# A DeltaNet recurrence and a low-rank mixer on one core: inverse times v added up in PSUM, 15 products for 18 in two more half chunks

## The chip, the cores and the metric

One Trainium2 chip, one of its cores. The metric is the device time of one execution in microseconds (us); less is better.

## The reference

Two blocks run one after the other. The first is a recurrence over 768 positions for 4 batches and 8 heads of 48 columns; its output, with the heads side by side (384 columns), is the input of a mixer.

```python
k_n = k / (norm(k) + 1e-6)
for t in range(768):                       # state: 4 x 8 x 48 x 48, starts at 0
    y[t]  = q[t] @ state
    v_old = state.T @ k_n[t]
    state = state + beta[t] * outer(k_n[t], v[t] - v_old)
x = y with heads side by side              # 4 x 768 x 384
u = x + (x.transpose @ U @ V).transpose    # U: 768 x 32, V: 32 x 768
out = u + relu(u @ w_ch1) @ w_ch2          # 384 -> 1536 -> 384
```

All is fp32.

## The kernel before

**The recurrence** is done in chunks of 64 positions, 12 chunks a batch, 6 chunks ("unit" n) at a time for all 8 heads. Within a chunk the kernel solves a triangular system: it forms the products of keys (`grams`, `products`), inverts 32x32 diagonal blocks on VectorE column by column (`blocks`, lines 824 and 830), and joins them into the inverse of a 64x64 block with small matmuls (`joins`, lines 881 to 942). `recur(b)` then uses that inverse `zt`. `prepare` multiplies it by the keys (line 1044, to `kq`) and by v (line 1055, back into `vn`), three chunks at a time. Each chunk c then takes four steps that hang on one another: 8 matmuls of `kq` with the state (line 1093); a VectorE subtraction z = `vn` - that product (line 1106); 8 matmuls of keys with z (line 1121); a VectorE addition to the state (line 1132). Beside the chain, `outputs` makes y from the queries with the state and the masked products with z (lines 1004 and 1018), which ScalarE copies to `X` (line 988). These matmuls use 64x64 tiles of TensorE's array, those of `joins` 32x32, those of the mixer 128x128.

**The mixer** goes over a batch in three chunks of 256 positions, (b, i). `front` adds the low-rank part and turns u to `ut` (lines 1488 to 1534). `wide` makes the 1536 hidden features: 6 pairs of feature tiles, each with 3 matmuls a tile of 256 columns (line 1596), and ScalarE applies the ReLU (line 1553). `narrow` multiplies by w_ch2 (line 1761) in 7 products for 8, from sums that VectorE makes (lines 1676 and 1683), and `gather` adds the results to `X` (line 1689). The last batch has its own code with 15 products for 18 in both layers, over 768 positions at once (lines 1402 and 1891).

**15 products for 18.** The first layer on 3 by 3 blocks of weights and 3 by 2 blocks of u (128 by 128 each) is 18 block products. A bilinear scheme does it with 15, from sums of weight blocks (`weight_sums`) and of u blocks (`tokens`). `FAST` names the chunks that do this: before, (2, 2) alone, both halves h of the features. `CHAINS` lists the products e in two chains; each runs through one PSUM region, where a product is added to the sum so far, and after each product the sum is read (`seen`): a ScalarE copy for some (line 1645 or 1640), a VectorE addition or subtraction for the others (line 1651). So the next product of a chain has to wait for the read. Each half h has one PSUM bank, with its two chains in the two halves of it, and every product is 2 matmuls of 128 columns (line 1626).

**The order.** The coroutines above don't choose when they run. `ORDER` is a long list that gives each step of each coroutine its place, and `run` emits the instructions in that order; every engine works its own queue in it. Costs in calls such as `op("pe", 0.23, "Q", ...)` are left from the planner that made the list. PSUM has four pairs of banks (`pair`); two banks of one of them become the mixer's (`mix`) later. Input loads go through the SP and GpSimd queues, weights through SP.

Of the kernel before, what the change touches and what calls it, by code (L numbers as in the profile page):

```python
# [8 lines left out]
FP32 = mybir.dt.float32  # L9
# [8 lines left out]
BK = 32  # L18
# [9 lines left out]
def kernel(  # L28
# [116 lines left out]
    add_up b0 i0 f00: 594 612 668; add_up b0 i0 f03: 632 645 667; add_up b0 i1 f00: 793 820 841; add_up b0 i1  # L145
    f03: 846 859 861; add_up b0 i2 f00: 1012 1041 1060; add_up b0 i2 f03: 1040 1042 1046; add_up b1 i0 f00: 1151
    1161 1173; add_up b1 i0 f03: 1208 1213 1214; add_up b1 i1 f00: 1347 1371 1372; add_up b1 i1 f03: 1357 1375
    1378; add_up b1 i2 f00: 1505 1574 1594; add_up b1 i2 f03: 1592 1595 1598; add_up b2 i0 f00: 1684 1685 1725;
    add_up b2 i0 f03: 1726 1728 1731; add_up b2 i1 f00: 1843 1849 1866; add_up b2 i1 f03: 1865 1871 1876; add_up
    b2 i2 f00: 2108 2110 2111; add_up b2 i2 f03: 2107 2109 2112; blocks n0: 61 73 75 76 82 84 86 88 89 91 93 94  # L150
    96 97 103 110 114 122; blocks n1: 143 157 160 163 173 175 179 192 201 206 208 212 213 215 218 219 226 229;
    blocks n2: 479 498 510 513 514 518 520 524 526 528 529 532 536 538 539 541 542 544; blocks n3: 691 708 710
    711 714 716 718 720 721 722 733 740 744 748 752 755 756 760 768 769 771 785 788 792 794 797 798 799 800 801
    802 824 825 826; blocks n4: 937 941 942 944 948 951 964 965 966 967 975 977 979 1011 1017 1022 1031 1036
    1039 1043 1045 1062 1078 1081 1082 1093 1099 1104 1117 1120 1122 1125 1127 1129; blocks n5: 1144 1152 1155
    1156 1159 1160 1165 1167 1168 1169 1187 1207 1230 1231 1233 1239 1241 1242 1243 1256 1260 1261 1265 1266
    1272 1274 1277 1278 1280 1313 1319 1350 1354 1355; blocks n6: 1469 1475 1476 1477 1478 1480 1481 1482 1483
    1499 1502 1516 1524 1526 1539 1548 1552 1558 1573 1588 1590 1597 1599 1603 1605 1606 1612 1617 1622 1623
    1635 1637 1638 1645; blocks n7: 1674 1686 1688 1691 1692 1693 1694 1705 1707 1709 1716 1721 1722 1746 1749
    1753 1756 1766 1774 1783 1784 1786 1795 1804 1822 1824 1825 1826 1827 1828 1830 1831 1851 1852; channels b0  # L160
    i0 e0: 546 547; channels b0 i0 e1: 551 552; channels b0 i0 e2: 553 555; channels b0 i0 e3: 556 567; channels
    b0 i0 e4: 568 588; channels b0 i0 e5: 597 600; channels b0 i1 e0: 738 743; channels b0 i1 e1: 759 761;
    channels b0 i1 e2: 775 778; channels b0 i1 e3: 796 805; channels b0 i1 e4: 822 829; channels b0 i1 e5: 830
    832; channels b0 i2 e0: 924 927; channels b0 i2 e1: 932 934; channels b0 i2 e2: 936 939; channels b0 i2 e3:
    960 972; channels b0 i2 e4: 992 994; channels b0 i2 e5: 995 1030; channels b1 i0 e0: 1110 1112; channels b1
    i0 e1: 1115 1116; channels b1 i0 e2: 1130 1132; channels b1 i0 e3: 1142 1146; channels b1 i0 e4: 1153 1154;
    channels b1 i0 e5: 1172 1180; channels b1 i1 e0: 1257 1258; channels b1 i1 e1: 1273 1286; channels b1 i1 e2:
    1287 1295; channels b1 i1 e3: 1299 1311; channels b1 i1 e4: 1315 1334; channels b1 i1 e5: 1340 1342;
    channels b1 i2 e0: 1451 1461; channels b1 i2 e1: 1465 1484; channels b1 i2 e2: 1485 1488; channels b1 i2 e3:
    1490 1501; channels b1 i2 e4: 1518 1519; channels b1 i2 e5: 1535 1549; channels b2 i0 e0: 1643 1647;  # L170
    channels b2 i0 e1: 1652 1672; channels b2 i0 e2: 1673 1677; channels b2 i0 e3: 1701 1702; channels b2 i0 e4:
    1703 1706; channels b2 i0 e5: 1710 1711; channels b2 i1 e0: 1797 1798; channels b2 i1 e1: 1813 1814;
    channels b2 i1 e2: 1834 1837; channels b2 i1 e3: 1839 1840; channels b2 i1 e4: 1841 1844; channels b2 i1 e5:
    1845 1846; cut f0 f00 k0 to1: 2205; cut f0 f00 k1 to0: 2236; cut f0 f00 k1 to1: 2179; cut f0 f00 k2 to0:
    2246; cut f0 f00 k2 to1: 2245; cut f1 f03 k0 to1: 2293; cut f1 f03 k1 to0: 2301; cut f1 f03 k1 to1: 2295;
    cut f1 f03 k2 to0: 2312; cut f1 f03 k2 to1: 2311; cut f2 f06 k0 to1: 2214; cut f2 f06 k1 to0: 2235; cut f2
    f06 k1 to1: 2239; cut f2 f06 k2 to0: 2234; cut f2 f06 k2 to1: 2244; cut f3 f09 k0 to1: 2252; cut f3 f09 k1
    to0: 2292; cut f3 f09 k1 to1: 2294; cut f3 f09 k2 to0: 2306; cut f3 f09 k2 to1: 2303; diagonals n0 h0: 188
    190 191 195 210 222; diagonals n0 h1: 167 169 171 176 181 186; diagonals n1 h0: 312 315 319 336 343 353;
    diagonals n1 h1: 290 292 303 338 349 358; diagonals n2 h0: 598 599 622 628 634 638; diagonals n2 h1: 647 651  # L180
    672 697 703 724; diagonals n3 h0: 863 890 891 892 893 899; diagonals n3 h1: 879 880 881 889 931 933;
    diagonals n4 h0: 1171 1178 1183 1189 1198 1199; diagonals n4 h1: 1163 1210 1211 1232 1246 1247; diagonals n5
    h0: 1373 1387 1392 1396 1419 1436; diagonals n5 h1: 1395 1407 1410 1415 1416 1417; diagonals n6 h0: 1699
    1734 1735 1736 1787 1788; diagonals n6 h1: 1655 1681 1764 1789 1790 1791; diagonals n7 h0: 1874 1879 1885
    1889 1906 1909; diagonals n7 h1: 1854 1856 1873 1888 1902 1905; fifteen b2 i2 h0 k0: 1953 1962 1977 1987
    2007 2016 2042 2055 2088; fifteen b2 i2 h0 k1: 1956 1991 2004 2008 2054 2082; fifteen b2 i2 h1 k0: 1960 1976
    2005 2011 2028 2063 2073 2089 2096; fifteen b2 i2 h1 k1: 1990 2017 2051 2072 2083 2097; front b0 i0: 495 502
    503 515 516 519; front b0 i1: 523 561 591 602; front b0 i2: 636 652 678 682; front b1 i0: 1056 1064 1074
    1080 1102 1105; front b1 i1: 1106 1114 1131 1164; front b1 i2: 1196 1219 1228 1238; front b2 i0: 1593 1596
    1601 1619 1627 1628; front b2 i1: 1632 1671 1690 1700; front b2 i2: 1737 1748 1762 1769; front b3 i0: 2094  # L190
    2095 2102 2103 2114 2117; front b3 i1: 2119 2121 2123 2124; front b3 i2: 2127 2129 2131 2132; gather b0 i0
    h0 c0 k0: 677; gather b0 i0 h0 c0 k1: 680; gather b0 i0 h0 c1 k6: 737 871; gather b0 i0 h1 c0 k2: 693;
    gather b0 i0 h1 c0 k5: 734 926; gather b0 i0 h1 c1 k3: 706; gather b0 i0 h1 c1 k4: 715; gather b0 i1 h0 c0
    k0: 862; gather b0 i1 h0 c0 k1: 847; gather b0 i1 h0 c1 k6: 916 925; gather b0 i1 h1 c0 k2: 873; gather b0
    i1 h1 c0 k5: 913 1034; gather b0 i1 h1 c1 k3: 876; gather b0 i1 h1 c1 k4: 887; gather b0 i2 h0 c0 k0: 1044;
    gather b0 i2 h0 c0 k1: 1071; gather b0 i2 h0 c1 k6: 1109 1428; gather b0 i2 h1 c0 k2: 1072; gather b0 i2 h1
    c0 k5: 1111 1450; gather b0 i2 h1 c1 k3: 1079; gather b0 i2 h1 c1 k4: 1087; gather b1 i0 h0 c0 k0: 1206;
    gather b1 i0 h0 c0 k1: 1216; gather b1 i0 h0 c1 k6: 1251 1780; gather b1 i0 h1 c0 k2: 1220; gather b1 i0 h1
    c0 k5: 1249 1445; gather b1 i0 h1 c1 k3: 1229; gather b1 i0 h1 c1 k4: 1240; gather b1 i1 h0 c0 k0: 1377;
    gather b1 i1 h0 c0 k1: 1388; gather b1 i1 h0 c1 k6: 1446 1664; gather b1 i1 h1 c0 k2: 1408; gather b1 i1 h1  # L200
    c0 k5: 1441 1630; gather b1 i1 h1 c1 k3: 1412; gather b1 i1 h1 c1 k4: 1413; gather b1 i2 h0 c0 k0: 1589;
    gather b1 i2 h0 c0 k1: 1604; gather b1 i2 h0 c1 k6: 1636 1832; gather b1 i2 h1 c0 k2: 1608; gather b1 i2 h1
    c0 k5: 1639 1781; gather b1 i2 h1 c1 k3: 1613; gather b1 i2 h1 c1 k4: 1620; gather b2 i0 h0 c0 k0: 1727;
    gather b2 i0 h0 c0 k1: 1733; gather b2 i0 h0 c1 k6: 1782 1968; gather b2 i0 h1 c0 k2: 1752; gather b2 i0 h1
    c0 k5: 1794 2309; gather b2 i0 h1 c1 k3: 1754; gather b2 i0 h1 c1 k4: 1768; gather b2 i1 h0 c0 k0: 1898;
    gather b2 i1 h0 c0 k1: 1897; gather b2 i1 h0 c1 k6: 1951 2197; gather b2 i1 h1 c0 k2: 1915; gather b2 i1 h1
    c0 k5: 1957 2369; gather b2 i1 h1 c1 k3: 1918; gather b2 i1 h1 c1 k4: 1938; gather b2 i2 h0 c0 k0: 2116;
    gather b2 i2 h0 c0 k1: 2120; gather b2 i2 h0 c1 k6: 2142 2367; gather b2 i2 h1 c0 k2: 2126; gather b2 i2 h1
# [1813 lines left out]
```

## Time and profile before

| | |
|---|---|
| three runs | 587.42, 589.74, 590.85 us; median 589.74 |
| profiled execution | 591.4 us, of which the core's span 589.5 |
| mean granted TensorE clock | 0.939 of full speed |
| busy: TensorE matmuls (PE) | 552.9 us, 94% |
| busy: weight loads (PEld), beside the matmuls | 479.6 us, 81% |
| busy: VectorE (DVE) | 449.8 us, 76% |
| busy: ScalarE (ACT) | 221.8 us, 38% |
| busy: GpSimd (POOL) | 133.1 us, 23% |
| DMA | 36.23 MB, mean 61 GB/s |

A group's row reads: line, engine, operation, out<-in by the program's names, shapes, xcount | busy us, mean ns of one | idle time of the engine before them and what ended it. A row of waits reads: who <- whom, us in total, times, longest. A row of the chain or the timeline begins with its start in us from the span's start and its length. A busy PE is one whose pipeline holds a matmul.

### The profile page before, as it was taken

To read this page: it belongs to the slowest core of one execution; us is meant where nothing else is said; L and a number is where in the kernel's file an instruction comes from. 1 tells how busy PE (TensorE), PEld (TensorE's weight loads), DVE (VectorE), ACT (ScalarE), POOL (GpSimd) and SP (SyncE) were. 2 spreads that over 40 slices of the span, in tenths; PEclk is the share of its full clock that TensorE was granted. 3 is DMA by queue.
4 is the path that set the end of the run, shared out by engine and by line. 5 is a ranking of instruction groups with operands and counts; after the bars stand their busy time and mean duration, and the time that the engine had idled before them with its cause. 6 is when DMAs were issued, how large, how long until landed. Compare 5 with 4: busy or idle time off the path is not lost.

```text
span 589.5 us, 23569 instructions
## 1 busy us (share of the span) xinstructions
PE 552.9 (94%) x10452; PEld 479.6 (81%) x10452; DVE 449.8 (76%) x1077; ACT 221.8 (38%) x460; POOL 133.1 (23%) x229
## 2 busy tenths in 40 slices
PE   3788886899999999999999999999999999999997
PEld 3788775688988988889989987989889777755996
DVE  3888756899999577989957489999858345799743
ACT  2846473616432632026325332143261442335100
POOL 8122034124206415032313403063310000000000
PEclk9665566999999999999999999999999999999999
DMA  9960638532206135030302403160210000100001
GB/s 143 200 158 24 217 86 186 109 94 49 37 2 121 22 65 105 12 68 15 67 19 51 85 13 72 34 130 17 68 29 4 17 4 1 40 2 0 1 27 68
DMA packets 89397, 36.23 MB, mean 61 GB/s; under 512 B 75408, under 2 KB 87056, under 8 KB 89296
## 3 DMA queue, kind: packets, MB, share of 16 engines
q1 hardware_dynamic: 80752, 24.69, 20.0%
q0 software_dynamic: 6944, 9.74, 7.7%
q8 instruction: 82, 1.34, 0.9%
q10 hardware_dynamic: 1600, 0.30, 0.3%
q14 instruction: 19, 0.16, 0.1%
HBM read 29.98 MB, written 4.72 MB: 59 GB/s over the span
## 4 chain that ended last, share of the span: by engine, by line
PE 82%; DVE 11%; issue 3%; ACT 2%; DMA 1%; SPq 0%; DVEq 0%; ACTq 0%
PE P L1761 22%; PE P L1596 20%; PE P L1891 7%; PE P L1402 7%; PE P L721 4%; PE P L1626 3%; PE P L1093 2%; DVE xt L830 2%; DVE prod L824 2%; PE P L1121 2%; PE P L895 2%; PE P L881 2%; PE P L1044 2%; PE P L1055 2%; PE P L1018 1%
## 5 line engine op out<-in xcount | busy, mean ns | idle before, releaser
L1596 PE MATMUL P<-ut,w_sb 128*128 128x256 f32 x576 | 133.4, 385 | 0.0
L1596 PEld LDWEIGHTS P<-ut,w_sb 128*128 128x128 f32 x576 | 106.6, 190 | 15.4 <-issue 0.6
L1761 PE MATMUL P<-w_sb,hs 128*128 128x192 f32 x540 | 94.5, 329 | 0.0
L1761 PEld LDWEIGHTS P<-w_sb,hs 128*128 128x128 f32 x540 | 87.4, 190 | 2.7 <-issue 1.8
L830 DVE TENSOR_TENSOR xt<-xt,prod 128x112 f32<-128x112 f32 (+21 forms) x200 | 64.6, 323 | 6.9
L824 DVE TENSOR_TENSOR prod<-gs,xt 128x112 f32<-128x112 f32 (+21 forms) x200 | 63.2, 316 | 3.5
L988 ACT COPY X<-P 64x192 f32<-64x192 f32 x96 | 30.0, 313 | 68.0 <-PE P L1018 67.1
L1553 ACT ACTIVATE hs<-P 128x512 f32<-128x512 f32 x48 | 28.6, 597 | 64.3 <-PE P L1596 55.4
L1761 PE MATMUL P<-w_sb,S 128*128 128x192 f32 x216 | 37.7, 330 | 0.0
L576 POOL DMA_DIRECT2D slot<-in_v_dram x32 | 21.1, 666 | 73.1 <-DVE prod L824 68.6
L1761 PEld LDWEIGHTS P<-w_sb,S 128*128 128x128 f32 x216 | 34.9, 190 | 2.6 <-issue 1.2
L1689 DVE TENSOR_TENSOR X<-X,P 128x192 f32<-128x192 f32 x63 | 21.7, 348 | 17.4 <-PE P L1761 17.1
L562 POOL DMA_DIRECT2D slot<-in_k_dram x40 | 24.9, 629 | 38.8 <-DVE z L1106 37.6
L1106 DVE TENSOR_TENSOR z<-slot,P 128x192 f32<-128x192 f32 x44 | 15.5, 352 | 23.7 <-PE P L1093 23.1
L960 ACT COPY slot<-zz 32x384 f32<-32x384 f32 x64 | 32.2, 508 | 3.0 <-DVE zz L899 2.1
L721 PE MATMUL P<-slot 48*64 48x64 f32 x1536 | 32.1, 237 | 0.7 <-DVE slot L752 0.7
L721 PEld LDWEIGHTS P<-slot 48*64 48x64 f32 x1536 | 29.1, 151 | 4.2 <-issue 1.6
L967 POOL MEMSET slot<- 32x384 f32 x32 | 13.0, 411 | 83.7 <-PE P L924 64.5
L576 POOL DMA_DIRECT2D slot<-in_k_dram x44 | 29.3, 668 | 7.8 <-PE P L1121 7.6
L562 POOL DMA_DIRECT2D slot<-in_q_dram x40 | 24.5, 618 | 16.3 <-DVE slot L734 8.2
L809 POOL MEMSET xt<- 128x1056 f32 x8 | 7.9, 982 | 83.4 <-DVE zz L837 83.3
L1132 DVE TENSOR_TENSOR s<-s,P 128x192 f32<-128x192 f32 x40 | 13.9, 348 | 12.2 <-PE P L1121 11.3
(204 smaller groups left out, 1053.9 us busy)
## 6 DMA issues: line engine op xcount, KB each, us to landing
w_sb<-in_moe_w_ch_dram SPq DMA_DIRECT2D x10, 384.0 KB, 4.8
out_dram<-X SPq DMA_DIRECT2D x19, 192.0 KB, 3.4
slot<-in_k_dram SPq DMA_DIRECT2D x48, 72.0 KB, 3.7
slot<-in_k_dram POOLq DMA_DIRECT2D x44, 72.0 KB, 3.5
slot<-in_v_dram SPq DMA_DIRECT2D x32, 72.0 KB, 3.0
slot<-in_v_dram POOLq DMA_DIRECT2D x32, 72.0 KB, 3.0
X<-in_moe_w_ch_dram SPq DMA_DIRECT2D x6, 384.0 KB, 4.6
wide<-in_moe_w_ch_dram SPq DMA_DIRECT2D x6, 384.0 KB, 5.2
```

The lines of the kernel that those rows point to most:

```text
L562: queue.dma_start(out=blocked(n)[quarter(y % 4), j, g, :, 0:w], in_=src[b, 4 * g + 2 * j + par, hf * UC * L : (hf + 1) * UC * L, BK * low ...
L576: queue.dma_start(out=t[half(1 - g if name == "z" else g), :, to, 0:D], in_=src[b, 4 * g + s, hf * UC * L : (hf + 1) * UC * L, :].rearrang ...
L721: nc.tensor.matmul(p_g[half(g ^ (par * i)), par, c], kq[rows, c, j, 0, half(g)], kq[rows, c, j, i, half(g)], start=True, stop=True,)
L824: nc.vector.tensor_tensor(out=prod, in0=gb[:, :, j : j + 1, j + 1 :].to_broadcast([128, split, m, w]), in1=xb[:, :, 0:m, j : j + 1].to_bro ...
L830: nc.vector.tensor_tensor(out=xb[:, :, 0:m, j + 1 :], in0=xb[:, :, 0:m, j + 1 :], in1=prod, op=ALU.subtract,)
L960: nc.scalar.copy(pg[quarter(i), :, at, :, a : a + BK], cut(zc, h)[quarter(i)].rearrange("p r (c j) t -> p r c j t", j=2),)
L988: nc.scalar.copy(x[half(c % 2), c // 2, 4 * D * g : 4 * D * (g + 1)].rearrange("p (j r d) -> p r j d", r=2, d=D), states(p_y)[half(g)],)
L1402: nc.tensor.matmul(to, forms[h][w][:, g] if isinstance(w, str) else w1_of(*w, h)[:, g], TOKENS[t] if isinstance(t, str) else u_of(*t), sta ...
L1553: nc.scalar.activation(hs[:, fs[0] : fs[1] + 1 : fs[1] - fs[0]], p_f, ACTF.Relu)
L1596: nc.tensor.matmul(p_f[:, x], w(x, t), ut[:, t], start=(t == 0), stop=(t == KT - 1))
L1761: nc.tensor.matmul(to, of[0], of[1], start=of[2], stop=of[3], skip_group_check=True)
L1891: nc.tensor.matmul(p[:, m], a[:, h, 128 * m : 128 * m + 128], v[:, h, j], start=fresh and m == h == j == 0, stop=(j == h == 1), skip_group ...
```

## The change

- **15 products for 18 in two more half chunks.** `FAST` also names half 0 of chunks (1, 2) and (2, 1). Their other half stays with plain matmuls.
- **One line to a bank.** In the chunk (2, 2), where both halves are fast, a chain now has a bank of its own and a product is 4 matmuls over all four feature groups of both halves, read by one instruction of 512 columns. In a half-fast chunk the chains use a pair of banks, one each, and a product is 2 matmuls as before. The chains are cut differently: products 10 and 12 are in the second.
- **Inverse times v in PSUM.** For batches 1 to 3, `prepare` no longer multiplies by v. A new coroutine `values(c)` writes the inverse times v of one chunk into a PSUM pair; the matmuls with the state, with `kq` negated, are added there; ScalarE copies the sum as z. The matmuls of keys with z go into other columns of the next chunk's pair.
- **Diagonal blocks.** For units 3 to 7, `products` builds `diag` with four ScalarE copies of 32 partitions in place of a ScalarE multiplication and two VectorE operations.
- **First pair of `narrow`.** In half-fast chunks its two products are made in the other order.
- **New order.** `ORDER` is a new list.

The core of the diff, without `ORDER`:

```diff
@@ products
-                yield op("act", act(384) + 0.1, rush=True)
-                nc.scalar.mul(to, p_g[:, :, :, 0:BK], even[:, 0:1])
-                for r in range(2):
+                if n > NU * JOINT:
+                    for y in range(4):
+                        a = BK * (y % 2)
+                        yield op("act", act(384))
+                        nc.scalar.copy(to[quarter(y)], p_g[quarter(y), :, :, a : a + BK])
+                else:
+                    yield op("act", act(384) + 0.1, rush=True)
+                    nc.scalar.mul(to, p_g[:, :, :, 0:BK], even[:, 0:1])
+                for r in range(2) if n <= NU * JOINT else ():
@@ recur
+    JOINT = 1
@@ prepare
+            if n >= NU * JOINT:
+                yield op("act", act(768), give=[("pair", x)])
+                nc.scalar.mul(
+                    kq[:, cs[0] : cs[2] + 1, :, 0].rearrange("p c j (g t) -> p (c j) g t", g=2),
+                    p_k.rearrange("p g c j t -> p (c j) g t"), -1.0,
+                )
+                emitted(("ready", n, h), 0.1)
+                return
@@ recur
+        def values(c):
...
+            x = yield op("pe", 0.23, "Q", take="pair", words=32, flow=0.16)
+            sums[c] = x
+            for j, par, g in heads:
+                nc.tensor.matmul(
+                    states(pair(x)[:, :, 0 : 2 * D])[half(g ^ par), par, j],
+                    zt[half(g), par, cu, j],
+                    vn[half(g), cu, 2 * par + j],
+                    start=(j == 0),
+                    stop=(c == 0),
+                    skip_group_check=True,
+                )
...
-            if c == 0:
+            if b >= JOINT:
+                yield need(("values", b, c))
+                xb = sums[c]
+                p_b = pair(xb)[:, :, 0 : 2 * D]
+                if c > 0:
...
+                            kq[half(par, D), cu, j, 0, half(g)],
+                            states(s_old)[half(par, D), g, j],
+                            start=False,
...
+                yield op("act", act(192), give=[("pair", xb)], rush=True)
+                z = zs[c] = small.tile([128, 4, D], FP32, name="z", bufs=3)
+                nc.scalar.copy(z.rearrange("p (r j) d -> p r (j d)", r=2), p_b)
...
+                if b >= JOINT:
+                    yield need(("values", b, c + 1))
+                    p_s = pair(sums[c + 1])[:, :, 2 * D : 4 * D]
@@ fast chunks
-    FAST = {(2, 2): (0, 1)}
+    FAST = {(1, 2): (0,), (2, 1): (0,), (2, 2): (0, 1)}
     CHAINS = (
-        ((4, 0, 1, 1), (10, 2, 0, -1), (12, 1, 0, 1), (13, 1, 0, 1), (2, 1, 1, -1), (7, 0, 1, -1), (14, 2, 1, 1),
-         (5, 2, 0, -1), (11, 0, 0, 1)),
-        ((1, 1, 1, 1), (6, 0, 1, 1), (9, 1, 1, 1), (0, 1, 0, -1), (3, 2, 0, 1), (8, 2, 1, -1)),
+        ((4, 0, 1, 1), (13, 1, 0, 1), (2, 1, 1, -1), (7, 0, 1, -1), (14, 2, 1, 1), (5, 2, 0, -1), (11, 0, 0, 1)),
+        ((1, 1, 1, 1), (10, 2, 0, -1), (12, 1, 0, 1), (6, 0, 1, 1), (9, 1, 1, 1), (0, 1, 0, -1), (3, 2, 0, 1),
+         (8, 2, 1, -1)),
     )
@@ fifteen
-        def fifteen(h, k):
-            bank = h if len(quickly) == 2 else 0
+        def fifteen(k):
+            joint = len(quickly) == 2
...
-                for g in range(2):
+                if z == 0:
+                    p = (mixed(k) if joint else pair(own[0])[:, k])[:, 0 : GT * len(quickly)]
+                    p = p.rearrange("p (g n) -> p g n", n=128)
+                for g in range(2 * len(quickly)):
+                    h = quickly[g // 2]
@@ seen
-                yield op("act", act(256), rush=True)
+                yield op("act", act(n), rush=True)
                 nc.scalar.mul(to, p, float(sign))
@@ narrow
+            turns = [(1, 1), (0, 0)] if e == 0 and len(quickly) == 1 else list(enumerate(ys))
```

More of the change, by code (lines that the diff above doesn't have):

```diff
@@ L1072, in prepare @@
             emitted(("ready", n, h), 0.1)
+        sums = {}
+        def values(c):
+            n, cu = NU * b + c // UC, c % UC
+            _, _, zt, _, _, vn, _, _ = units[n]
+            yield need(
+                *[x for h in [cu // 3] for x in (("upper", n, h), ("diagonal", n, h))],
+                ("grams", n), ("scaled", n), *[("placed", b, c - 2)] * (c > 1),
+            )
[9 more added lines that the diff above has]
+                    skip_group_check=True,
+                )
+            emitted(("values", b, c))
         zs = {}
+        if b >= JOINT:
+            for c in range(NC):
+                begin(values(c), 60)
         for u in range(NU):
@@ L1618, in fifteen @@
                     *[("weights", 2 + y) for y in range(len(PAIRS))],
-                    *[("w1 sums", h)] * isinstance(w, str),
+                    *[("w1 sums", h) for h in quickly] * isinstance(w, str),
                     *[("sum", b, i, int(x[1:])) for x in [t] if isinstance(x, str)],
-                    *[("seen", b, i, h, CHAINS[k][z - 1][0])] * (z > 0),
-                    *{6: [("made", b, i, h, 13)], 13: [("made", b, i, h, 1)]}.get(e, []),
-                )
-                yield op("pe", 0.432, "F", take=("mix", bank) if z == k == 0 else None, words=8)
@@ L1625, in fifteen @@
-                for g in range(2):
+                    *[("seen", b, i, CHAINS[k][z - 1][0])] * (z > 0),
+                )
+                got = yield op(
+                    "pe", 0.432 * len(quickly), "F", words=8 * len(quickly),
+                    take=None if z or k and not joint else ("mix", k) if joint else "pair",
+                )
+                if z == 0 and not joint:
+                    own[0] = own[0] if k else got
+                if z == 0:
+                    p = (mixed(k) if joint else pair(own[0])[:, k])[:, 0 : GT * len(quickly)]
+                    p = p.rearrange("p (g n) -> p g n", n=128)
@@ L1631, in fifteen @@
                     )
-                emitted(("made", b, i, h, e))
-                begin(seen(h, e, p, r, m, sign, [("mix", bank)] * (e == 11)), 3)
-        def seen(h, e, p, r, m, sign, give):
-            to = hs[:, HF * h + r : HF * h + r + 4 : 3, 128 * m : 128 * m + 128]
+                emitted(("made", b, i, e))
+                give = [("mix", k)] if joint and e in (8, 11) else [("pair", own[0])] if e == 11 else []
+                begin(seen(e, p, r, m, sign, give), 3)
+        own = [None]
```

542 lines of the change are left out of this document (284 added, 258 removed).

## The prediction

> **What bounds the kernel now.** I read the page first (share of each engine and the chain), then the stages, then who waits for whom, then single matmuls in the timeline. All from one execution of 591.4 us: a span of 589.5 and 1.9 around it, 1.7 above the median of the runs shown (589.74). I work the sum as a difference against the profiled execution and carry it to the median.
>
> ```profile
> PE 552.9 (94%) x10452; PEld 479.6 (81%) x10452; DVE 449.8 (76%) x1077; ACT 221.8 (38%) x460; POOL 133.1 (23%) x229
> ...
> PE 82%; DVE 11%; issue 3%; ACT 2%; DMA 1%; SPq 0%; DVEq 0%; ACTq 0%
> ...
> 0.00:20.00 20.00, 9.31 (x199) 8.48 (x200) 9.21 (x30) 7.20 (x14) 14.93 (x31) 1.00 1.09 156
> ...
> 120.00:140.00 20.00, 19.74 (x456) 16.80 (x455) 19.53 (x40) 7.25 (x14) 8.38 (x14) 1.00 0.37 86
> 140.00:160.00 20.00, 20.00 (x550) 18.27 (x549) 19.50 (x45) 10.48 (x20) 5.52 (x10) 1.00 0.22 39
> ...
> 460.00:480.00 20.00, 18.46 (x566) 16.28 (x564) 8.12 (x24) 8.56 (x25) 0.00 (x0) 1.00 0.02 4
> ```
>
> The stages give busy us of PE, PEld, DVE, ACT, POOL, then the granted clock. Batch 0 of the recurrence and the weight loads fill the first 115 us with PE waiting; from 120 us on PE is busy for nearly all of every 20 us at a granted clock of 1.00. DVE is almost as full around 120 to 160. What PE still waits for after 112 us:
>
> ```profile
> PE P L1093 <- DVE s L1132: 0.8, 1, 0.8
> PE P L1531 <- DVE X L1512: 0.8, 1, 0.8
> PE P L1626 <- ACT hs L1645: 0.7, 2, 0.5
> PE P L1507 <- DVE tt L1494: 0.4, 1, 0.4
> PE P L1626 <- DVE hs L1651: 0.3, 1, 0.3
> PE P L881 <- DVE zz L837: 0.3, 1, 0.3
> PE P L1121 <- DVE z L1106: 0.3, 1, 0.3
> ...
> PEld P L1121 <- DVE z L1106: 2.9, 12, 0.4
> ```
>
> 3.6 us in all. So from 115 us on only less work on PE, or fewer breaks in it, moves the end. The orders of instructions of the two kernels are equal on PE up to this point (the first 1314 matmuls), so the first 114 us stand as they are.
>
> **The change part by part. Products.** One fp32 matmul stands in the trace as two records.
>
> ```profile
> 415.84 2.79 PE P L1596 x12
> ...
> 420.82 13.15 PE P L1596 x60
> ...
> 456.33 0.71 PE L1626 MATMUL P<-S,w_sb 128*128 128x128 f32 x4
> 457.56 1.60 PE L1626 MATMUL P<-S,w_sb 128*128 128x128 f32 x12 [0.52 <-ACT hs L1645]
> 459.10 0.45 PE L1093 MATMUL P<-s,slot 48*64 48x48 f32 x16
> 459.37 0.41 PE L1004 MATMUL P<-s,slot 48*64 48x48 f32 x16
> 459.60 0.41 PE L1018 MATMUL P<-z,slot 64*64 64x48 f32 x16
> 460.02 0.40 PE L1121 MATMUL P<-z,slot 64*48 64x48 f32 x16
> 460.35 0.71 PE L1626 MATMUL P<-S,w_sb 128*128 128x128 f32 x4
> ```
>
> From x60 and x12: (13.15-2.79)/48 = 0.216 us for a record of 256 columns. From the x12 and x4 of L1626: (1.60-0.71)/8 = 0.111 for 128 columns. Each of the two new half-fast chunks drops 18 matmuls of 256 columns (36 records, 7.8 us) and gets 30 of 128 (60 records, 6.7 us): -1.1 each, **-2.2 us**. The least is -0.7: that holds if each of the 15 runs of 8 records pays 0.1 more for its first load. The joint chunk b2 i2 keeps its 60 matmuls.
>
> The Trainium skill ("TensorEngine Tiling (Array Packing)", Instruction Overhead) speaks against more, shorter matmuls: about 60 cycles of overhead on each. At its 2.4 GHz that is 25 ns, and 48 more records would cost 1.2 us by it, so -1.0 here. The rows show 2 x 0.111 against 0.216, 6 ns a record, and I go by them.
>
> **Changes of tile size.** In the instruction orders PE goes 175 times from one tile size (128x128, 64x64, 32x32, 128x32) to another before, and 160 times after. A run of 12 records of 256 columns takes 2.79 where 12 x 0.216 is 2.59: 0.20 for its entry and exit. The small groups next to it: L1004 to L1018 is 0.23 start to start, L1121 to L1626 0.33, L1093 to L1004 0.27: 0.14 more. So 0.34 for two changes, some 0.15 for one (0.10 to 0.20): 15 x 0.15 = **-2.2 us**, all on PE's path.
>
> **One line to a bank, and the stalls of b2 i2.** A chain's product used to cover two feature groups of one half and now covers all four, so behind a product twice as much matmul time stands while its sum is read. The 0.7 and 0.3 above are PE waiting for exactly these reads; I take **-0.7**, with 0 and -1.0 as ends. A read becomes 512 wide; it is one instruction for two, so ACT and DVE lose fixed cost.
>
> **Tail.** The new order has three places where nothing stands between a matmul and the read it needs. In the first layer of the last batch, product 12 comes right behind product 10 of the same line twice; before, other lines lay between. In its second layer the last product's second half comes behind a DVE read of its first half.
>
> ```profile
> L1427 ACT ACTIVATE slot<-P 128x384 f32<-128x384 f32 x20 | 9.3, 490 | 18.5 <-PE P L1402 18.5
> L1645 ACT ACTIVATE hs<-P 128x256 f32<-128x256 f32 x10 | 3.6, 384 | 10.0 <-PE P L1626 9.2 <-ACT X L988 0.8
> L1900 DVE TENSOR_TENSOR X<-X,P 128x384 f32<-128x384 f32 x14 | 7.7, 552 | 14.7 <-PE P L1891 14.7
> L1689 DVE TENSOR_TENSOR X<-X,P 128x192 f32<-128x192 f32 x63 | 21.7, 348 | 17.4 <-PE P L1761 17.1
> ```
>
> The nearest row is the uncovered wait of L1626 above: 0.52 idle around a copy of 0.384. With 0.490 that is 0.63, twice 1.3; with a DVE read of 0.348 it is 0.49. The last read is then half as wide (0.552 to 0.348, -0.2). Together **+1.6** (1.0 to 2.2).
>
> **Recurrence, batches 1 to 3.** The inverse times v is no longer made ahead and copied (12 copies of L1068 go); 8 matmuls a chunk write it into PSUM, 8 more subtract the state's share there, and ACT copies z where DVE subtracted. PE's count is the same, 288 matmuls with v for 288. DVE loses 33 subtractions.
>
> ```profile
> L1106 DVE TENSOR_TENSOR z<-slot,P 128x192 f32<-128x192 f32 x44 | 15.5, 352 | 23.7 <-PE P L1093 23.1 <-ACT hs L1645 0.4
> L988 ACT COPY X<-P 64x192 f32<-64x192 f32 x96 | 30.0, 313 | 68.0 <-PE P L1018 67.1
> L1063 ACT COPY slot<-P 128x768 f32<-128x768 f32 x16 | 12.8, 798 | 24.8 <-PE P L1044 24.5
> L1068 ACT COPY slot<-P 128x576 f32<-128x576 f32 x16 | 10.3, 642 | 0.9 <-PE P L1055 0.7
> L1553 ACT ACTIVATE hs<-P 128x512 f32<-128x512 f32 x48 | 28.6, 597 | 64.3 <-PE P L1596 55.4 <-issue 6.7 <-DVE slot L734 2.0
> L948 ACT ACTIVATE slot<-P 32x384 f32<-32x384 f32 x32 | 15.3, 480 | 7.7 <-PE P L942 7.3
> L731 ACT ACTIVATE slot<-P,even 128x384 f32<-128x384 f32 x16 | 9.1, 582 | 27.1 <-PE P L721 26.9
> L734 DVE SCALAR_TENSOR_TENSOR slot<-P,even,slot 128x192 f32<-128x192 f32 x32 | 12.3, 412 | 7.7 <-ACT slot L731 7.6
> ```
>
> A step of the chain (state matmuls, z, S matmuls, state) is as long as before: a copy of about 0.31 for a subtraction of 0.35. DVE: -33 x 0.352 = -11.6. Units 3 to 7 also build their diagonal blocks with four ACT copies (0.48 each) in place of one ACT and two DVE (0.582, 2 x 0.412): DVE -8.2, ACT +13.4, and the block's transpose starts 1.92 - 1.41 = 0.5 later, beside work of batches that PE has queued. The new token sums and reads of the half chunks put some 14 back on DVE (about 34 operations of 0.4, between the 0.348 and 0.552 of the 192 and 384 wide forms above). Net DVE -6, ACT +20. ACT, busy for 38%, hides that, if the queue in front of z is short; PE's own sum is **0**. Its ends: -2.9, if all twelve waits of the weight load for z go, and +7.2: in ACT's new order a 768-wide copy stands straight ahead of 6 copies of z and a 512-wide ReLU ahead of 4 (6 x 0.80 + 4 x 0.60).
>
> **Sum.** -2.2 - 2.2 - 0.7 + 1.6 = **-3.5**: 587.9 for the profiled execution, 586.2 for the median. A measurement of this kernel can tell about 0.5% (2.9 us) from no change.
>
> **The rivals.** First, **slower: z waits in ACT's queue.** In the 33 steps z now stands behind ReLUs and copies of other stages; the S matmuls wait, and PE behind them in order. For it: the rows of L1063 and L1553 are two to three times a z copy. Against it: ACT is idle for 62%, DVE for 24%, so z left the fuller queue. With +7.2 the sum is +3.7, 593.4. It decides from (3.5+2.9)/33 = 0.19 us a step.
>
> Second, **DVE was holding PE back** (19.5 of 20 us in two stages): relieved of 6 us it lets the waits of 3.6 and of 2.9 go too, half of each: -6.8, 582.9. Against it: PE's waits are few as they are.
>
> Third, **the gain is given back**: a PE that is earlier waits for the block solves on DVE in 120 to 180 us, which are no shorter; 0, 589.7.
>
> Fourth, **the halves don't pay**: the 128-wide records average 0.155, as the 56 in 8.7 us of one group do, since short runs pay an entry each time:
>
> ```profile
> L1626 PE MATMUL P<-S,w_sb 128*128 128x128 f32 x56 | 8.7, 286 | 0.6 <-ACT hs L1645 0.5
> ```
>
> 120 x 0.155 = 18.6 against 15.6, +3.0 for -2.2: the sum is +1.7, 591.4, and with the upper tail (+0.6) and a 0 for the joint chunk (+0.7) +3.0, 592.7. Against it: most new runs have four matmuls next to other 128x128 matmuls, so no entry is paid.
>
> **How the numbers follow.** Forecast 0.47 (583.5 to 588.7 by itself), z on ACT 0.15, DVE relieved 0.18, given back 0.13, halves don't pay 0.07. Faster by over 0.5%, below 586.8: the second rival and 0.30 of the forecast, 0.48. Slower, above 592.7: the first and fourth, 0.22. Within: the rest of the forecast and the third, 0.30. The lower end adds the best bounds, -2.2 - 3.0 - 1.0 + 1.0 - 2.9 = -8.1: 581; the upper the z rival with the poor ends of products (-0.7), switches (-1.5), joint chunk (0) and tail (+2.2), +7.2: 597; I draw it in to 596, since they hardly all meet.
>
> **What would show it.** PE's busy time between 115 us and the end shorter by 3 to 4 us; records of the products 0.111 apart in the two half chunks; two idle gaps of some 0.6 us near the start of the last batch's first layer and one before the last matmuls; no growth of waits of the S matmuls, now for ACT. It is wrong if PE's waits after 112 us rise above 8 us: z copies queued on ACT would show it, waits for block solves the third rival, and records 0.15 apart the fourth.

## The result, and the profile after

| | before | after |
|---|---|---|
| first comparison, median (runs) | 590.36 us (8) | 587.14 us (8) |
| ratio, 95% interval | | 0.9944 [0.9917, 0.9971] |
| second comparison, median (runs) | 589.2 us (29) | 585.23 us (12) |
| ratio, 95% interval | | 0.995 [0.9925, 0.9975] |
| profiled execution, span | 589.5 us | 583.8 us |

The forecast was 586.2 us, 3.5 less than before; the two comparisons give 3.2 and 4.0 less. By the ratios that is 0.5 to 0.6%, right at the bound of what was taken as distinguishable; in both comparisons the 95% interval lies below 1. The page of the changed kernel: engines, then the chain by engine.

```profile
PE 547.7 (94%) x10500; PEld 478.3 (82%) x10500; DVE 445.6 (76%) x1049; ACT 240.0 (41%) x519; POOL 132.5 (23%) x229
...
PE 84%; DVE 8%; ACT 3%; issue 3%; DMA 1%; SPq 0%; DVEq 0%; ACTq 0%
```

PE is as full as before and still the bound. DVE is 4 us lighter, ACT 18 heavier, about as worked out (6 and 20). What PE waits for after 112 us, all rows:

```profile
PE P L1479 <- ACT slot L1504: 1.2, 2, 0.6
PE P L1673 <- ACT ut L1611: 0.9, 1, 0.9
PE P L908 <- issue: 0.6, 2, 0.3
PE P L1980 <- DVE X L1989: 0.4, 1, 0.4
PE P L1141 <- DVE s L1211: 0.4, 1, 0.4
PE P L1584 <- DVE tt L1571: 0.4, 1, 0.4
PE P L952 <- ACT zz L942: 0.3, 1, 0.3
PE P L1033 <- ACT z L1155: 0.2, 1, 0.2
```

4.4 us in all, of which the first row and the fourth are the tail's three gaps. The waits at the products of the joint chunk (L1626 before, L1711 now) are gone. z, now a copy by ACT, is waited for once, for 0.2 us. A wait for `ut` of 0.9 is new and was not foreseen; it stands at 116 us, where PE before waited 0.8 at L1531.

The starts of matmul records cut the span into stages. "Order starts to differ" is the first matmul that the new order moves; the columns "again" and "tail moved" belong to the first experiment below.

| us | before | after | again | tail moved |
|---|---|---|---|---|
| start to where the order starts to differ | 115.04 | 113.11 | 115.29 | 111.82 |
| from there to the last batch's first layer (the middle stage) | 392.22 | 386.92 | 386.66 | 387.49 |
| first layer of the last batch | 38.77 | 40.61 | 40.61 | 39.32 |
| its second layer | 38.84 | 39.55 | 39.55 | 39.55 |
| last matmul to the end | 4.61 | 3.59 | 3.60 | 3.59 |

The first line is the same instructions in every column: it ran from 110.95 to 115.29 us over the twelve executions profiled here, which is as much as the change itself. The 1.9 us that the profiled pair differ by there are no effect of the change. The middle stage repeats to about 1 us in the changed kernel (the kernel before was profiled once), and it is the one to read. Cut at its own ends, it shows what PE did in it: stage, length, then busy us of PE, PEld, DVE, ACT, POOL, granted clock, DMA; first before, then again.

```profile
115.04:507.26 392.22, 388.19 (x7557) 339.84 (x7550) 309.71 (x770) 138.18 (x291) 96.03 (x161) 1.00 0.22 45
115.29:501.95 386.66, 384.54 (x7605) 340.60 (x7598) 304.84 (x743) 157.10 (x350) 96.11 (x161) 1.00 0.22 46
```

PE is busy for 3.7 us less (3.8 in the first profile, 384.34) and idle for 2.12 us (2.58) in place of 4.03.

### The profile page after: what moved, and what is told of

Read it like the earlier page. It is cut to its first block, busy times and chain, and to the rows that moved or that the text cites. A ratio compares the mean times of both kernels' runs of the same rounds, so it can differ in the third digit from the quotient of the medians.

```text
span 583.8 us, 23666 instructions
## 1 busy us (share of the span) xinstructions
PE 547.7 (94%) x10500; PEld 478.3 (82%) x10500; DVE 445.6 (76%) x1049; ACT 240.0 (41%) x519; POOL 132.5 (23%) x229
## 4 chain that ended last, share of the span: by engine, by line
PE 84%; DVE 8%; ACT 3%; issue 3%; DMA 1%; SPq 0%; DVEq 0%; ACTq 0%
PE P L1851 20%; PE P L1673 20%; PE P L1479 7%; PE P L1980 7%; PE P L1711 5%; PE P L728 4%; PE P L1019 2%; PE P L1033 2%; PE P L1141 2%; PE P L1109 2%; PE P L908 2%; PE P L894 2%; PE P L1584 2%; PE P L1197 2%; PE P L1059 2%
## 5 line engine op out<-in xcount | busy, mean ns | idle before, releaser
L1673 PE MATMUL P<-ut,w_sb 128*128 128x256 f32 x504 | 118.0, 385 | 0.9 <-ACT ut L1611 0.9
L1673 PEld LDWEIGHTS P<-ut,w_sb 128*128 128x128 f32 x504 | 92.8, 190 | 14.3 <-ACT ut L1611 1.1
L843 DVE TENSOR_TENSOR xt<-xt,prod 128x112 f32<-128x112 f32 (+21 forms) x200 | 64.5, 323 | 6.9
L837 DVE TENSOR_TENSOR prod<-gs,xt 128x112 f32<-128x112 f32 (+21 forms) x200 | 63.5, 317 | 3.7
L1630 ACT ACTIVATE hs<-P 128x512 f32<-128x512 f32 x42 | 24.9, 597 | 33.9 <-PE P L1673 31.0
L728 PE MATMUL P<-slot 48*64 48x64 f32 x1536 | 30.7, 231 | 2.0 <-issue 1.2
L728 PEld LDWEIGHTS P<-slot 48*64 48x64 f32 x1536 | 27.7, 144 | 5.5 <-issue 2.2
L1155 ACT COPY z<-P 128x192 f32<-128x192 f32 x36 | 11.4, 317 | 43.5 <-PE P L1141 43.4
L1740 DVE TENSOR_TENSOR hs<-hs,P 128x256 f32<-128x256 f32 (+1 forms) x27 | 13.5, 507 | 17.6 <-PE P L1711 16.8
```

The source lines that it names most:

```text
L728: nc.tensor.matmul(p_g[half(g ^ (par * i)), par, c], kq[rows, c, j, 0, half(g)], kq[rows, c, j, i, half(g)], start=True, stop=True,)
L837: nc.vector.tensor_tensor(out=prod, in0=gb[:, :, j : j + 1, j + 1 :].to_broadcast([128, split, m, w]), in1=xb[:, :, 0:m, j : j + 1].to_bro ...
L843: nc.vector.tensor_tensor(out=xb[:, :, 0:m, j + 1 :], in0=xb[:, :, 0:m, j + 1 :], in1=prod, op=ALU.subtract,)
L1673: nc.tensor.matmul(p_f[:, x], w(x, t), ut[:, t], start=(t == 0), stop=(t == KT - 1))
```

## Experiments

"The changed kernel" is at 585.23 us, ratio 0.995, below. Kernels were compared with the kernel before on the same chip; its medians in the three groups were 589.2, 589.26 and 588.69.

### The tail: three exchanges in the order

> The changed kernel itself, to have it on one chip beside the others. Every reading of the change expects 0.990 to 0.998 of the kernel before (the first comparison gave 0.9944), 584 to 589 us. Its trace also tells which gaps come again: the two of about 0.6 us in the first layer of the last batch and the one of about 0.45 us before the last matmuls should, if they belong to the order and not to one execution.

> The changed kernel with three entries of its written order exchanged in the last batch, the same instructions otherwise: the third product of line f0 changes places with the quick product of f2 behind it, and the quick product of f0 comes ahead of the third product of f3, so that a product no longer takes a PSUM bank right behind the matmul whose sum ACT has still to read there. Theory of the prediction (the two gaps of 0.63 and 0.58 lie on PE's path, nothing else is late there): the two gaps go, 1.2 us shorter than the changed kernel (0.6 to 1.6), about 586 where that one has 587.1; first layer of the last batch 39.4 us instead of 40.6. Rival, the gaps are only where PE's lead over ACT is spent and come back behind another instruction: less than 0.3 us of difference, first layer 40.3 us or more.

```diff
 ORDER, by place
-2207 short f0 k3      2208 quick f2
+2207 quick f2         2208 short f0 k3
-2251 short f3 k2      2252 read e4 f3      2253 quick f0
+2251 quick f0         2252 short f3 k2     2253 read e4 f3
```

Again: 585.23 us. Moved: 583.85 us, ratio 0.9918 [0.9893, 0.9943]. The timeline of PE (start, length, engine, line, operation, shapes, records, idle before) in the changed kernel, at the start of the first layer, and at the end of the second:

```profile
501.32 0.81 PE L1479 MATMUL P<-slot,w_sb 128*128 128x384 f32 x2
502.76 2.20 PE L1479 MATMUL P<-slot,w_sb 128*128 128x384 f32 x6 [0.63 <-ACT slot L1504]
...
515.28 0.91 PE L1479 MATMUL P<-slot,w_sb 128*128 128x384 f32 x2 [0.58 <-ACT slot L1504]
...
579.60 0.92 PE L1980 MATMUL P<-w_sb,slot 128*128 128x192 f32 x4 [0.45 <-DVE X L1989]
```

With the entries exchanged the first two are gone: the records now follow without a break, here the place of the first one.

```profile
499.96 0.81 PE L1479 MATMUL P<-slot,xt 128*128 128x384 f32 x2
500.60 3.00 PE L1479 MATMUL P<-slot,w_sb 128*128 128x384 f32 x8
```

The layer falls from 40.61 to 39.32 us, 1.3 for two gaps of 0.63 and 0.58: they were on the path and nothing else stood behind them. The medians differ by 1.4, less than the intervals of the two ratios are wide, so it is the stage that shows it. This version has the lowest time here.

### The products: fewer halves, and one more

> The changed kernel with the halved products taken away again in the two chunks that the change gave them (second batch's last chunk, third batch's middle chunk): their second halves go through 18 products of 256 columns, one line to a bank, as the first halves do; 48 matmuls fewer, tile changes on PE 160 as in the changed kernel, the rest of the order as it was. Theory of the prediction (records of 0.216 and 0.111 us): 2.2 us slower than the changed kernel (0.7 to 2.9), of which up to 0.7 for VectorE or ScalarE work that is then no longer needed could be hidden; PE's busy time +2.2. Rival, the halves don't pay because short runs pay an entry each time (0.155 us a record): 3.0 us faster; halfway, 0, if half of the entries are paid.

```diff
-    FAST = {(1, 2): (0,), (2, 1): (0,), (2, 2): (0, 1)}
+    FAST = {(2, 2): (0, 1)}
```

589.75 us, ratio 1.0008 [0.999, 1.0026]: 4.5 slower than the changed kernel, twice what the products' price gives. Besides this line, the entries of the two chunks in `ORDER` are others, and `run` here holds a step back until what it needs is there. The middle stage says which part is which: 391.80 against 386.66, +5.1. PE's waits after 112 us rose from 3.4 (again) to 6.1; the stage, and the longest waits outside the tail, in the line numbers of this kernel:

```profile
112.90:504.70 391.80, 387.03 (x7556) 339.80 (x7549) 294.85 (x709) 152.82 (x334) 96.12 (x161) 1.00 0.22 46
...
PE P L981 <- issue: 1.1, 1, 1.1
PE P L1702 <- ACT ut L1640: 0.9, 1, 0.9
PE P L1138 <- ACT ut L1640: 0.8, 1, 0.8
```

PE is idle for 4.77 us of the stage against 2.12, so 2.6 of the 5.1 are waits. The second row of waits stood at 0.9 in the changed kernel too; the first, a pause that the profile gives no releaser for, and the third are new, in an order that was laid out for other products. The other 2.5 are work of PE, 387.03 against 384.54: the products, forecast at 2.2. The estimate from the 60 cycles of the Trainium skill ("TensorEngine Tiling (Array Packing)", Instruction Overhead) was 1.0 for them, so the run speaks for the rows. The records of the new products in the changed kernel, at (1.05 - 0.61)/4 = 0.11 us each, say the same:

```profile
411.10 1.05 PE L1711 MATMUL P<-S,w_sb 128*128 128x128 f32 x8
...
413.29 0.61 PE L1711 MATMUL P<-S,power 128*128 128x128 f32 x4
```

"The halves don't pay" is refuted: it had this kernel faster by up to 3.0.

> The kernel with the two gaps of the last batch removed, and beyond that the halved products in the first half of one more chunk (third batch's first), in an order that I spread there by hand: 18 matmuls of 256 columns fewer in it, 30 of 128 columns in their place, token sums and reads of the halves on VectorE and ScalarE more. By the price of the products alone: 1.1 us faster than the kernel with the gaps removed (583.85), about 582.8. Rival, what decides is whether the order hides the sums and the reads that each product waits for: PE then waits for them at this chunk's products, 3 to 10 us slower than it, and the products' own gain does not show.

```diff
+    FAST = {(1, 2): (0,), (2, 0): (0,), (2, 1): (0,), (2, 2): (0, 1)}
```

The products go in by hand beside the other work, and `run` holds steps back as above. 595.94 us, ratio 1.0105 [1.0074, 1.0136]: 12.1 slower than the version with the tail moved. The middle stage is 9.4 longer (396.93 against 387.49), and PE's waits are 11.8 against 3.2, 8.6 more. The two longest rows (L1752 is the halved product here):

```profile
PE P L1752 <- DVE hs L1781: 4.3, 3, 2.3
PE P L1752 <- DVE X L1630: 1.5, 1, 1.5
```

In the first row a product waits for the read of the one before it in its chain. The products' own 1.1 does not show either: PE is busy for 385.30 us of this stage against 384.37. So this run doesn't show that a further chunk can pay; it shows that it doesn't in an order that has no other matmuls for such waits.

### The price of a change of tile size

> The changed kernel with one more matmul, one column wide and 64x64, in the middle of 63 of its plain products of 128x128 (the 192-wide ones of the second matrix); it writes into a column of the bank that nothing reads. PE's changes of tile size go from 160 to 286, 126 more; everything else is the same. The prediction's price of a change, 0.15 us (0.10 to 0.20) on PE's path, gives 126 x 0.15 = +18.9 us (12.6 to 25.2), and 63 matmuls of two records of some 0.02 give 2.5 more: 21 us slower than the changed kernel (15 to 28). Rival, a change costs nothing by itself and the 15 fewer changes brought nothing: 2 to 4 us slower. Between them, at 0.09 (what is left of the stretch before the last batch when the products are taken at their price and the waits as measured): +14.

```diff
                         nc.tensor.matmul(
                             to, of[0], of[1], start=of[2], stop=of[3], skip_group_check=True
                         )
+                        if f == 2:
+                            nc.tensor.matmul(
+                                mixed(x)[half(0), HD : HD + 1], ident[half(0), half(0)],
+                                ident[half(0), 0:1], start=False, stop=True, skip_group_check=True,
+                            )
```

616.51 us, ratio 1.0478 [1.044, 1.0516]: 31 slower, more than the range for 0.15 and far from the 2 to 4 of the rival. The timeline around one insertion, and granted clocks in a stretch (stage, length, busy us of PE, PEld, DVE, ACT, POOL, granted clock, DMA):

```profile
470.46 1.14 PE L1851 MATMUL P<-w_sb,hs 128*128 128x192 f32 x6
471.53 0.27 PE L1855 MATMUL P<-ident 64*64 64x1 f32 x2
471.74 1.24 PE L1851 MATMUL P<-w_sb,hs 128*128 128x192 f32 x6
```
```profile
281.99 0.21 PE L955 MATMUL P<-zz 32*32 32x32 f32 x1 [1.77 <-issue]
```
```profile
282.00:284.00 2.00, 2.00 (x16) 1.96 (x16) 0.33 (x1) 1.61 (x4) 2.00 (x5) 0.56 0.13 31
284.00:286.00 2.00, 2.00 (x8) 1.55 (x8) 0.00 (x0) 0.71 (x2) 1.82 (x3) 0.50 0.31 68
286.00:288.00 2.00, 2.00 (x8) 2.00 (x7) 0.89 (x3) 0.00 (x0) 0.00 (x0) 0.50 0.21 57
288.00:290.00 2.00, 2.00 (x10) 1.55 (x10) 0.19 (x1) 0.00 (x0) 0.00 (x0) 0.74 0.00 0
```

Records of 192 columns stand 0.163 apart. 470.46 to 471.74 is 1.28 where six records take 0.98, and the six behind take 1.24 where such a run without an entry takes 1.14: 0.40 for two changes and two records of one column, which start 0.08 apart. So a change is 0.16 to 0.20. Over 63 places that is 25.2 us. The middle stage is 33.2 longer; PE's waits are 8.0 against 3.4, 4.6 of it, nearly all pauses in which PE waited for nothing that the profile shows; and after the 1.77 us pause above the clock stands near half for 6 us and more, 2 x (0.44 + 0.50 + 0.50 + 0.26) = 3.4. 25.2 + 4.6 + 3.4 = 33.2. The price was right, for changes between 128x128 and 64x64; the pauses and what the clock did after one of them were not in the expectation. Another pause of 1.69 us in this run (L952, at 324 us) left the clock at 1.00.

### z back on VectorE, and the diagonal blocks back

> The changed kernel with one edit: in batches 1 to 3 VectorE copies z out of PSUM in place of ScalarE; order and all else the same. VectorE gets about 33 copies of 0.35 us more (about +12 us), ScalarE loses as many of 0.32. Theory of the prediction (neither engine's queue in front of z reaches PE's path; the recurrence is worth 0): within 1 us of the changed kernel, PE's waits after 112 us still 4 to 6 us. Rival, z waits in ScalarE's queue behind long ReLUs and copies: 1 to 7 us faster than the changed kernel, and fewer waits of the S matmuls. Rival, VectorE was holding PE back and the change relieved it: 3 us slower or more, since VectorE gets all of its 6 us back and 6 more, with PE waiting for VectorE in the recurrence and the block solves.

```diff
-                yield op("act", act(192), give=[("pair", xb)], rush=True)
+                yield op("dve", dve(192), give=[("pair", xb)], rush=True)
...
-                nc.scalar.copy(z.rearrange("p (r j) d -> p r (j d)", r=2), p_b)
+                nc.vector.tensor_copy(out=z.rearrange("p (r j) d -> p r (j d)", r=2), in_=p_b)
```

601.2 us, ratio 1.0215 [1.0185, 1.0245]: 16 slower. My own theory had within 1 and fell. One place, first DVE, then PE, and three stretches of 40 us with busy time and clock:

```profile
286.14 0.42 DVE L837 TENSOR_TENSOR prod<-gs,xt 128x256 f32<-128x256 f32 x1
286.60 0.42 DVE L843 TENSOR_TENSOR xt<-xt,prod 128x256 f32<-128x256 f32 x1
286.94 0.35 DVE L1155 COPY z<-P 128x192 f32<-128x192 f32 x1
```
```profile
285.87 0.45 PE L1109 MATMUL P<-slot 64*64 64x48 f32 x16
287.35 0.45 PE L1033 MATMUL P<-z,slot 64*64 64x48 f32 x16 [1.03 <-DVE z L1155]
```
```profile
260.00:300.00 40.00, 37.32 (x648) 33.64 (x648) 33.81 (x84) 15.79 (x32) 16.03 (x26) 0.96 0.24 57
300.00:340.00 40.00, 38.20 (x741) 33.71 (x740) 24.84 (x61) 13.45 (x29) 7.80 (x14) 0.95 0.13 23
340.00:380.00 40.00, 37.28 (x844) 32.45 (x846) 30.27 (x84) 16.02 (x39) 12.68 (x21) 0.96 0.29 52
```

z stands behind the column-by-column inversion (L837, L843); DVE is busy for 33.8 us of the 40 in which this lies. PE's waits rose from 3.4 to 15.6, 12.2 more. The middle stage rose by 18.5; much of the rest is again the granted clock of the three stretches, 40 x (0.04 + 0.05 + 0.04) = 5.2.

This says that z does not fit into DVE's queue in this order. It doesn't say that DVE held the kernel before back: there DVE had the subtraction and PE's waits were 3.6 us, in an order laid out for it. Whether that order had to give up something for it stays open; the change alone on the old order was not tried.

> The changed kernel with one part undone: the diagonal blocks of units 3 to 7 are again made by one ScalarE and two VectorE instructions each in place of four ScalarE copies; z stays on ScalarE and the order is the same but for the ten steps that fall away. VectorE gets back about 8 us, ScalarE loses about 13. Theory, VectorE's queue is what the recurrence and the block solves hang on (z on VectorE cost 16 us for 12 us more of VectorE work): 3 to 10 us slower than the changed kernel, PE's waits for VectorE after 112 us up by as much. Rival, it is z alone that must not stand behind VectorE's other work, and VectorE's load as such is hidden (the prediction's reading of an idle quarter): within 1.5 us.

```diff
-                if n > NU * JOINT:
+                if n > 99:
...
-                for r in range(2) if n <= NU * JOINT else ():
+                for r in range(2):
```

589.9 us, ratio 0.9999 [0.998, 1.0018]: 4.7 slower, the middle stage +4.1, waits +2.1. That is the number of the first theory, by another mechanism: one place carries it. DVE, then PE:

```profile
209.29 0.42 DVE L747 SCALAR_TENSOR_TENSOR slot<-P,even,slot 128x192 f32<-128x192 f32 x1 [4.64 <-ACT slot L744]
209.63 0.34 DVE L1778 TENSOR_TENSOR X<-X,P 128x192 f32<-128x192 f32 x1
209.89 0.35 DVE L1209 TENSOR_TENSOR s<-s,P 128x192 f32<-128x192 f32 x1
```
```profile
210.29 0.45 PE L1141 MATMUL P<-s,slot 48*64 48x48 f32 x16 [1.68 <-DVE s L1209]
```
```profile
210.00:212.00 2.00, 1.71 (x34) 1.53 (x35) 1.75 (x5) 0.72 (x3) 0.20 (x1) 0.65 0.03 3
212.00:214.00 2.00, 2.00 (x6) 1.55 (x6) 0.00 (x0) 0.92 (x2) 2.00 (x4) 0.50 0.54 84
```

The restored DVE instruction waits 4.64 us for ACT at the head of DVE's queue with the state's addition behind it. DVE was idle, not loaded, so this run doesn't show that DVE's load is what counts. After the 1.68 us pause as much again is lost: the clock is at 0.65 and 0.50 for 4 us, 2 x (0.35 + 0.50) = 1.7.

### How much of a delay of z reaches PE

> The changed kernel with each of the 36 copies of z in batches 1 to 3 made by two ScalarE instructions of 96 columns in place of one of 192, behind each other: the whole z is there some 0.17 us later (two of about 0.24 for one of 0.32), VectorE is not touched. Theory of the prediction (a step of the recurrence has other matmuls ahead of its S matmuls that hide a short delay; it decides only from 0.19 us a step): under 2 us slower than the changed kernel. Rival, the recurrence is PE's path and any delay of z comes out whole: 36 x 0.17 = 6 us slower.

```diff
+                to = z.rearrange("p (r j) d -> p r (j d)", r=2)
+                for y in range(2):
+                    nc.scalar.copy(to[:, y], p_b[:, y])
```

586.23 us, ratio 0.9943 [0.992, 0.9967]: no difference by the runs, and +1.3 in the middle stage (387.94). But the delay was mis-sized: two copies of 96 columns overlap and take 0.38 together where one takes 0.32, so z came only 0.06 later. Hence two runs with a real delay:

> The changed kernel with one more ScalarE copy of 128x192 out of the same PSUM bank ahead of each of the 36 copies of z in batches 1 to 3, into a spare tile that nothing reads. It waits for the same matmuls as z, so z is there some 0.27 us later (what such copies stand apart when they follow each other), above the 0.19 us a step from which the prediction let the first rival decide. That point took every microsecond as coming out whole: 36 x 0.27 = 9.7 us slower than the changed kernel by it. The other reading, PE has other queued work ahead of the S matmuls in most steps and only some steps come out: 1 to 5 us slower, the waits of the S matmuls (L1019, L1033, L1197 of the changed kernel) for ScalarE up by the same.

> The same with two such copies ahead of each z, about 0.54 us later. If every step comes out whole: 19 us slower than the changed kernel. If a step has some slack of its own that the first copy used up: more than twice what one copy costs, 4 to 12 us. If ScalarE's load alone mattered (36 x 0.54 = 19 us more of it, at 41% busy) and z's place did not: under 1 us, the same as with one.

```diff
+                for y in range(1):          # 2 in the other kernel
+                    spare = small.tile([128, 4, D], FP32, name="spare", bufs=1)
+                    nc.scalar.copy(spare.rearrange("p (r j) d -> p r (j d)", r=2), p_b)
                 nc.scalar.copy(z.rearrange("p (r j) d -> p r (j d)", r=2), p_b)
```

| copies ahead | z later by | x 36 | middle stage, against 386.66 | waits of PE | ratio |
|---|---|---|---|---|---|
| none | 0 | 0 | 0 | 3.4 us | 0.995 [0.9925, 0.9975] |
| one | 0.21 us | 7.7 | +4.7 | 7.1 us | 1.0005 [0.9981, 1.0029] |
| two | 0.56 us | 20.3 | +12.9 | 14.8 us | 1.0165 [1.0132, 1.0199] |

588.92 and 599.88 us. The longest of PE's waits for z with two copies ahead:

```profile
PE P L1109 <- ACT z L1158: 3.9, 7, 0.6
PE P L1019 <- ACT z L1158: 2.2, 5, 0.6
PE P L1200 <- ACT z L1158: 2.1, 4, 0.6
...
PE P L1033 <- ACT z L1158: 1.2, 2, 0.8
```

The delays are what the traces show; 0.27 and 0.54 were expected. About 0.6 of the delay comes out, at 0.21 as at 0.56, with a stage that repeats to about 1 us. That fits no slack that the first 0.2 us would use up, but steps of which some have much cover and others none. L1109 is the multiplication by v, which does not need z of its step; by the code the PSUM pair that it writes is given back by z's copy. ACT's load as such does not count: that reading had the two kernels equal.

## Why the prediction was right, point by point

The products, the price of a change of tile size and the three gaps came as worked out. That the total came within 0.5 us of the forecast is in part luck, as the points on the joint chunk, the recurrence and the tail show.

- **Products, -2.2.** 2.5 us of PE's work when they are undone. The order adds something that the prediction did not have: undone, they leave 2.6 of uncovered waits.
- **Changes of tile size, 15 x 0.15 = -2.2.** 0.16 to 0.20 measured for one between 128x128 and 64x64, so -2.4 to -3.0. That is the price times the count; no run put the 15 back.
- **Joint chunk, -0.7.** Mis-sized: between 456 and 490 us PE waited 2.1 us before, the 0.7 and 0.3 at its products and also 0.8 at L1093 and 0.3 at L1121, and no wait is listed there after and again. The sum took the first two alone. Other waits, new ones among them, take part of it back: in the whole middle stage the listed waits went from 3.1 to 2.4 (after) and 1.8 (again), PE's idle time from 4.0 to 2.6 and 2.1. One line to a bank was not tried by itself, so what it has of this, and what the new order has, stays open.
- **Recurrence, 0.** Not shown. The middle stage moved by -5.3 and -5.6; the forecast for it was -2.2 - 2.2 - 0.7 = -5.1. But the terms under it are off by about 1 each way. The kernel without the halves has the 15 fewer changes and the new recurrence, and PE is busy only 1.2 us less in it than before (387.03 against 388.19), where the changes alone were to bring 2.2. With the 2.4 to 3.0 of their measured price, something gives 1.2 to 1.8 back: the recurrence, or the rest of the new order; no run takes them apart. The idle time brought 1.5 to 1.9 in place of 0.7. That the two cancel is luck.
- **Tail, +1.6.** First layer +1.84, second +0.71, end -1.02, in sum +1.53. The gaps came to 0.63, 0.58 and 0.45 where 0.63, 0.63 and 0.49 were worked out. The account of the first two was wrong, though: it is not product 12 behind product 10 of one line, but another line's first product that takes the PSUM bank of the product just issued and has to wait for its read. Place and price held because the same copy ends the wait. That the last wide read is half as wide now was put at -0.2; the end came 1.0 nearer. The other 0.8 the sum left out: the last transfer to the output is smaller too. It is issued by L1915 before and by L2009 after; KB, and us from issue to landing:

```profile
out_dram<-X SPq DMA_DIRECT2D x1, 384.0 KB, 2.5
...
out_dram<-X SPq DMA_DIRECT2D x2, 96.0 KB, 1.6
```

  Against it stand breaks that the sum did not have either. Some 0.55 of the first layer (39.32 without the gaps, 38.77 before) are smaller breaks that I did not separate, and the second layer has 0.26 beside its gap. So the three gaps were right, and +1.53 for +1.6 is luck: what was left out on the one side cancels what was left out on the other.
- **First rival, z waits in ACT's queue.** It did not happen: one wait of 0.2 us. ACT stood idle ahead of z, 43.5 us over 36 copies, for matmuls:

```profile
L1155 ACT COPY z<-P 128x192 f32<-128x192 f32 x36 | 11.4, 317 | 43.5 <-PE P L1141 43.4
```

  Its point of decision was too low: it took each microsecond as coming out whole, where 0.6 does. With 0.21 us a step the kernel was not slower than before by 2.9 us but equal to it. The path itself is as sensitive as the rival needed: 0.56 a step made it 1.65% slower than before.
- **Second rival, DVE was holding PE back.** Not borne out: -6.8 was its sum, -3.2 and -4.0 came. Its reason has something to it: z on DVE cost 16 us in the new order. The change could not have used this order with z where it was.
- **Third rival, the gain is given back.** The block solves cost no gain: PE is busy for 19.43 and 20.00 us of the two stages of 20 (19.74 and 20.00 before), and the middle stage kept its 5.3.

```profile
120.00:140.00 20.00, 19.43 (x505) 16.29 (x504) 19.22 (x40) 5.54 (x11) 9.81 (x15) 1.00 0.44 87
140.00:160.00 20.00, 20.00 (x494) 18.33 (x493) 18.58 (x43) 13.75 (x28) 5.43 (x10) 1.00 0.10 22
```

- **Fourth rival, the halves don't pay.** Refuted by the kernel without them.

Of what was named beforehand to show the steps: PE's busy time after 115 us fell from 466.2 to 461.4 us (463.7 again), 4.7 and 2.5 where 3 to 4 was said, since the start shifts under that mark (in the middle stage it fell by 3.8 and 3.7); the three gaps stood where they were put; PE's waits after 112 us stayed under 8.

## What to carry to other kernels

On a PE that is full, count what its queue holds: records by length, changes of tile size, and the places where a product has to wait for a read; the sum came out within 1 us here, though single terms were off by as much and cancelled. An order written by hand is part of the kernel: taking products out without laying it out anew cost 5.1 us where the work is 2.5, and putting more in cost 9.4 where 1.1 was to be gained, the rest new waits. Give a copy on a tight chain to the engine that idles ahead of it, and look at what stands at the head of a queue, not only at the engine's load.

## What the runs showed of the hardware that was not expected

- **A pause of PE can be paid twice, and its length alone does not decide it.** After pauses of 1.68 and 1.77 us the granted clock fell from 1.00 to between 0.50 and 0.74 for 4 to 8 us, 1.7 and 3.4 us on top. But pauses of 1.69 us (the kernel with more changes, before 324 us), of 2.28 us (the kernel with one more half, 396 to 398 us) and of 1.03 us (at 287 us with z on DVE) left it at 1.00, the column behind the five engines:

```profile
322.00:324.00 2.00, 0.49 (x48) 0.38 (x33) 1.97 (x4) 1.14 (x3) 1.95 (x5) 1.00 0.04 11
...
396.00:398.00 2.00, 0.07 (x1) 0.00 (x0) 1.86 (x10) 0.00 (x0) 0.00 (x0) 1.00 0.01 4
```

  What decides it is not shown. The Trainium skill ("TensorE: Matmul & The Clock Gate", Part 1) tells of a gate that halves the clock after an idle window of about 3.4 us. The half agrees with the 0.50 here, but two pauses half as long were enough.
- **Two ScalarE copies of 96 columns cost 0.06 us more than one of 192**, 0.38 against 0.32, since the second starts before the first is done.
- **The start varies by itself.** The same first instructions took 110.95 to 115.29 us in twelve executions, which is why a change of 0.6% had to be read from stages.
